# Half token tiles whose two parts share one stationary operand, and one expert's gathered rows turned later

## The chip, the cores and the metric

The kernel runs on one core of one Trainium2 chip. The time is device microseconds (us) of one execution; a run's figure is the median of several. Engines are named as in the profile: PE (TensorE matmul), PEld (its weight loads), DVE (VectorE), ACT (ScalarE), POOL (GpSimd) and SP (SyncE, which issues most DMAs).

## The reference

Three layers follow one another. A banded attention (2 batches, 8 heads, 768 tokens, 64 values a head) gives x of 2 x 768 tokens with 512 values each. A mixing layer with one hidden layer of 2048 changes x. The last layer sends each token to one of 8 experts, chosen by a gate, and the change touches only this one:

```python
for b in range(B):
    for s in range(S):
        ...
        h = np.maximum(x[b, s] @ w1[e], 0.0)      # 512 -> 1024
        out[b, s] = p[e] * (h @ w2[e])            # 1024 -> 512
```

## The kernel before

Every matrix product of the last two layers is made of three products. A number is kept as two parts, a high one (`xh`, `wh`, `hh`) and a low one (`xl`, `wl`, `hl`, the rest), and `three` (L601 to L604) adds high x high, high x low and low x high into one PSUM tile.

The experts are handled in ten positions one after the other: two filler positions (-2 and -1), then positions 0 to 7. `WIDTHS` fixes how many tokens each of the positions 0 to 7 has: 192, 256, 128, 192, 128, 192, 128, 192. `TILES` counts the tiles of 128 tokens that cover them, so widths of 192 and 256 have two tiles. For a width of 192 the second tile begins at token 64 (`at_tile`, L1109): tokens 64 to 127 are computed in both tiles and stored twice with the same values.

A position has four units (`NP2`), and each unit has two chunks c of 128 of the 1024 hidden values, so a position has eight chunks f. One chunk of a position with two tiles goes through `e_gemm1` (L844): twelve matmuls into `g`, weights stationary and 192 or 256 tokens moving, and then `split_relu` (ACT writes `hh`, DVE writes `hl`). One chunk later `out_` (L1256) multiplies hh and hl, as stationary operands, with 512 columns of the second weights: three matmuls of 512 columns per tile, into the accumulators z of tile 0 and z of tile 1. A position of one tile (width 128) works otherwise: x is stationary, the hidden values are turned on PE (`turn_`, L1214), copied by ACT (L1218) and subtracted by DVE (L1219), and six matmuls of 512 columns follow.

Around a position stand these steps, in the order written in `before` (L1160) and in `unit` (L1197):
- `listed` and `gathered` read the list of tokens and gather their rows of x by an indirect DMA that POOL issues (L803). `gathered(pos + 1)` is called in the first unit of position pos.
- `turned` (L1137, `split_x` L807) turns one gathered tile on PE (four transposes, L810), copies it (ACT, L813) and subtracts (DVE, L814). In the third unit of pos it turns tile 0 of pos + 1, in the fourth unit tile 1.
- `weights` loads 1 MB for each unit of the next position (L820), and `split_ew` cuts weights into two parts (ACT L837, DVE L840), four steps for each unit, handed out between other work.
- `done` (L1147) stores a position: `store` (L857) scales an accumulator on ACT (L861) and scatters its rows to the output by an indirect DMA of POOL (L862). The tile framework makes each scatter to the output wait until the scatter before it has landed.

In position 7 the second products of the chunks f = 4 to 7 are put off to the end of the program (L1334 to L1338), behind a branch that skips `past_tiles`: tile 0 with twelve matmuls and its store, then tile 1 with twelve and its store.

Of the kernel before, what the change touches and what calls it, by code (L numbers as in the profile page):

```python
# [22 lines left out]
P = 128  # L23
# [46 lines left out]
def tile_kernel(ctx, tc, q, k, v, nn, U, V, w12, wg, wgt, ew, masks, lst0, out, dbg=None):  # L70
# [736 lines left out]
    def split_x(xg, t, xh, xl, ps, nm, at=None):  # L807
# [8 lines left out]
    e_hl = {}  # L816

# [25 lines left out]

    def e_gemm1(key, f, w, xh, xl, between, room=None):  # L844
        wh, wl = e_hl[key, f // 2]
        c = f % 2
        hh, hl = room or [ep.tile([P, 256], F32R, tag=t, bufs=3, name=f"{t}{key}{f}") for t in ("ehh", "ehl")]
# [6 lines left out]
        split_relu(hh[:, :w], hl[:, :w], g[:, :w])  # L854
        return hh, hl

    def store(acc, idx, prob):  # L857
# [3 lines left out]
        nc.scalar.mul(ot, acc, prob)  # L861
# [247 lines left out]
    def at_tile(pos, t):  # L1109
        return min(P * t, WIDTHS[pos] - P)  # L1110

    def listed(pos):
# [9 lines left out]
        if WIDTHS[pos] % P:  # L1122
            for t in range(n):
                read_list(nc.sync.dma_start(ids[:, t], lst[ds(s_of[pos] + at_tile(pos, t), P), :]))
# [4 lines left out]
    def gathered(pos):  # L1129
        ids = ex[pos]  # L1130
        idc = ep.tile([P, 2], I32, tag="idc", bufs=3, name=f"idc{pos}")
        xh = ep.tile([P, KC, 256], F32R, tag="xh", name=f"xh{pos}")
        xl = ep.tile([P, KC, 256], F32R, tag="xl", name=f"xl{pos}")
        xs = [gather(ids[:, t, 0:1], idc[:, t:t + 1], x2d) for t in range(TILES[pos])]
        ex[pos] = ids, xh, xl, xs

    def turned(pos, t):  # L1137
        if t < TILES[pos]:
            ids, xh, xl, xs = ex[pos]
            split_x(xs[t], t, xh, xl, side_tile, f"{pos}{t}", at_tile(pos, t))  # L1140
# [6 lines left out]
    def done(pos, tiles=None):  # L1147
# [4 lines left out]
        else:  # L1152
            ids = ex[pos][0]
            for t in tiles or range(TILES[pos]):
                store(accs[pos][t], ids[:, t, 0:1], ids[:, t, 1:2].bitcast(F32))
# [4 lines left out]
    def before(pos, p):  # L1160
        if pos >= 0:
# [8 lines left out]
            if pos + 1 < E and p >= 2:  # L1170
                turned(pos + 1, p - 2)
# [25 lines left out]
    def unit(pos, p, key, xh, xl, n, acc_):  # L1197

        wh, wl = e_hl[key, p]
        if n == 1:  # L1200
# [10 lines left out]
            hh = ep.tile([P, 256], F32R, tag="ehh", bufs=3, name=f"ehh{key}{p}")  # L1211
            hl = ep.tile([P, 256], F32R, tag="ehl", bufs=3, name=f"ehl{key}{p}")
# [237 lines left out]
```

## Time and profile before

| what | value |
|---|---|
| median of 3 runs | 607.74 us (605.58 to 607.93) |
| the profiled execution, its own time | 607.19 us |
| its span, first to last instruction | 605.3 us |
| PE busy | 582.0 us, 96% of the span |
| DVE, ACT, POOL busy | 416.8, 292.0, 128.1 us |
| mean granted TensorE clock | 0.993 of full speed |
| positions 0 to 7 | from about 443 us to the end |

The time of an execution is its span and 1.9 us around it. PE is busy nearly throughout; in the expert positions it stands still in two places only. An engine's busy time counts the stretches in which it has an instruction under way; matmuls overlap in the records, so what one costs is the distance from its start to the start of the next.

### The profile page before, as it was taken

To read this page: it belongs to the slowest core of one execution; us is meant where nothing else is said; L and a number is where in the kernel's file an instruction comes from. 1 tells how busy PE (TensorE), PEld (TensorE's weight loads), DVE (VectorE), ACT (ScalarE), POOL (GpSimd) and SP (SyncE) were. 2 spreads that over 40 slices of the span, in tenths; PEclk is the share of its full clock that TensorE was granted. 3 is DMA by queue.
4 is the path that set the end of the run, shared out by engine and by line. 5 is a ranking of instruction groups with operands and counts; after the bars stand their busy time and mean duration, and the time that the engine had idled before them with its cause. 6 is when DMAs were issued, how large, how long until landed. Compare 5 with 4: busy or idle time off the path is not lost. (4 is left out here: it accounts for less than half of the span.)

```text
span 605.3 us, 9730 instructions
## 1 busy us (share of the span) xinstructions
PE 582.0 (96%) x3469; PEld 518.1 (86%) x3469; DVE 416.8 (69%) x998; ACT 292.0 (48%) x631; POOL 128.1 (21%) x119
## 2 busy tenths in 40 slices
PE   8999999899999999999998999999899999999994
PEld 5999899789988899899997889877788989999993
DVE  5789986476899883448999445568624677595850
ACT  4877877633432342332222125425424677685841
POOL 5010030112213333333330211012330313031101
PEclk9999999989999999999999999999999999999998
DMA  8956651003323310250100028034295578868400
GB/s 216 311 157 198 217 172 50 2 5 134 140 91 118 140 69 1 88 191 36 36 18 0 1 65 317 37 122 157 54 359 199 178 266 323 275 244 310 167 15 35
DMA packets 35850, 83.47 MB, mean 138 GB/s; under 512 B 5631, under 2 KB 17791, under 8 KB 33744
## 3 DMA queue, kind: packets, MB, share of 16 engines
q1 hardware_dynamic: 31632, 70.87, 35.2%
q0 software_dynamic: 2784, 7.62, 3.5%
q10 hardware_dynamic: 1376, 4.26, 1.9%
q8 instruction: 29, 0.48, 0.3%
q14 instruction: 29, 0.24, 0.1%
HBM read 74.34 MB, written 8.77 MB: 137 GB/s over the span
## 5 line engine op out<-in xcount | busy, mean ns | idle before, releaser
L607 ACT ACTIVATE hh<-g 128x384 fp32r<-128x384 f32 x62 | 30.3, 489 | 109.0 <-PE g L604 108.5
L608 DVE SCALAR_TENSOR_TENSOR hl<-g,hh 128x384 fp32r<-128x384 f32 x62 | 34.5, 556 | 48.6 <-ACT hh L607 48.3
L338 PE MATMUL s<-kt,q 128*128 128x232 f32 (+1 forms) x192 | 55.2, 370 | 2.3 <-DVE m L348 1.7
L352 ACT ACTIVATE e<-t,m 128x232 f32<-128x232 f32 (+1 forms) x96 | 45.6, 476 | 18.2 <-DVE m L348 17.7
L675 DVE CUSTOM_DVE_ANT_0 sq_w<-x,wgt 128x512 f32<-128x512 f32 x54 | 47.1, 872 | 1.4
L348 DVE CUSTOM_DVE_ANT_0 t<-s,bias 128x232 f32<-128x232 f32 (+1 forms) x96 | 36.0, 377 | 17.2 <-PE s L338 7.2
L217 ACT ACTIVATE sq_w<-w 128x512 f32<-128x512 f32 x32 | 21.5, 672 | 48.9 <-DVE wf L224 48.9
L862 POOL DMA_INDIRECT out_dram<-x,ids x13 | 13.6, 1048 | 121.5 <-ACT x L861 100.6
L365 ACT COPY et<-pt 128x256 f32<-128x256 f32 (+1 forms) x96 | 33.5, 349 | 6.0 <-PE pt L362 3.8
L362 PE MATMUL pt<-ident,e 128*128 128x128 f32 x176 | 35.0, 273 | 0.0
L338 PEld LDWEIGHTS s<-kt,q 128*128 128x128 f32 x192 | 29.7, 191 | 5.4 <-DVE m L348 3.9
L222 DVE SCALAR_TENSOR_TENSOR wf<-w,wf 128x512 int32<-128x512 int32 x32 | 32.5, 1017 | 0.8
L382 PE MATMUL o<-v,et 128*128 128x65 f32 x160 | 30.9, 275 | 0.0
L783 POOL DMA_INDIRECT lst<-tab,slot x12 | 12.6, 1047 | 78.2 <-DVE tab L779 77.1
L608 DVE SCALAR_TENSOR_TENSOR ehlr<-egr,ehhr 128x192 fp32r<-128x192 f32 (+1 forms) x28 | 10.6, 377 | 26.1 <-ACT ehhr L607 26.1
L362 PEld LDWEIGHTS pt<-ident,e 128*128 128x128 f32 x176 | 24.1, 142 | 4.3 <-ACT et L365 0.5
L381 PE MATMUL o<-v,et 104*128 104x65 f32 x160 | 26.9, 249 | 0.0
L220 DVE SCALAR_TENSOR_TENSOR wf<-w,wf 128x512 int32<-128x512 int32 x32 | 25.6, 800 | 1.1 <-DVEq L463 0.7
L381 PEld LDWEIGHTS o<-v,et 104*128 104x128 f32 x160 | 24.2, 191 | 0.8
L382 PEld LDWEIGHTS o<-v,et 128*128 128x128 f32 x160 | 24.3, 191 | 0.0
L607 ACT ACTIVATE ehhr<-egr 128x192 fp32r<-128x192 f32 (+1 forms) x28 | 9.7, 347 | 29.1 <-PE egr L604 27.6
L224 DVE SCALAR_TENSOR_TENSOR wf<-sq_w,wf 128x512 f32<-128x512 f32 x32 | 22.1, 691 | 1.7
(777 smaller groups left out, 1935.8 us busy)
## 6 DMA issues: line engine op xcount, KB each, us to landing
ew<-in_ew_dram SPq DMA_DIRECT2D x32, 1024.0 KB, 6.4
w<-in_w_dram SPq DMA_DIRECT2D x16, 1024.0 KB, 4.8
v<-in_v_dram SPq DMA_DIRECT2D x8, 704.0 KB, 5.2
ew<-in_ew_dram ACTq DMA_DIRECT2D x4, 1024.0 KB, 11.7
x2d<-x SPq DMA_DIRECT2D x12, 256.0 KB, 2.0
kt<-in_k_dram SPq DMA_DIRECT2D x7, 408.0 KB, 4.1
q<-in_q_dram SPq DMA_DIRECT2D x14, 192.0 KB, 4.5
wgt<-in_wgt_dram SPq DMA_DIRECT2D x4, 512.0 KB, 4.3
```

The source lines that it names most:

```text
L220: nc.vector.scalar_tensor_tensor(t, low, 29, t, ALU.logical_shift_right, ALU.bitwise_or)
L222: nc.vector.scalar_tensor_tensor(t, high, -0x40000000, t, ALU.bitwise_and, ALU.bitwise_or)
L338: nc.tensor.matmul(s[:, :w], qs[n % 2][:, c], kt[:, kc], start=True, stop=True)
L348: nc.vector.tensor_tensor_reduce(out=t[:, :w], in0=s[:, :w], in1=bias[:, h, b0:b0 + w], scale=-0.125, scalar=3.0e38, op0=ALU.add, op1=ALU. ...
L352: nc.scalar.activation(e[:, :w], t[:, :w], AF.Exp, bias=m, scale=-1.0)
L362: nc.tensor.transpose(pt[:, P * j:P * j + P], e[:, c0:c0 + P], ident)
L365: nc.scalar.copy(et[:, :w], pt[:, :w])
L381: nc.tensor.matmul(oo, et[0:REST, 0:P], vt[0:REST, NT + i - 1, vc], start=True, stop=False)
L382: nc.tensor.matmul(oo, et[:, P:256], vt[:, i, vc], start=False, stop=True)
L607: nc.scalar.activation(hi, src, AF.Relu)
L608: nc.vector.scalar_tensor_tensor(lo, src, 0.0, hi.bitcast(F32), ALU.max, ALU.subtract)
L675: nc.vector.tensor_tensor_reduce(out=sq_w, in0=x_t[0, i], in1=rooms[k % 2][:, DM * j:DM * j + DM], scale=1.0, scalar=0.0, op0=ALU.mult, op ...
```

## The change

Positions with 192 tokens (0, 3, 5 and 7) get a second tile of 64 tokens in place of one of 128. Its list, its gather, its four transposes, its copy and subtraction and its store are of 64 rows (`tile_rows`). The two parts hh and hl of a chunk now lie in one tile `hl2` of 512 columns: hh in the first 192, the hl of tile 0 from column 256, and the hl of the half tile directly behind its hh, in columns 192 to 255. So the half tile's 64 columns of hh and 64 of hl are one stationary operand of 128 columns: `both` multiplies it with the high weights in one matmul (hh x high into rows 0 to 63 of the accumulator, hl x high into rows 64 to 127), and a second matmul with a stationary operand of 64 columns adds hh x low weights to rows 0 to 63. The two halves of the accumulator are added at the store: ACT copies the lower half, DVE adds, DVE scales, and POOL scatters 64 rows. The hl of 192 tokens is written by two DVE instructions (128 and 64 columns). At the end of the program the half tile is now multiplied and stored first, the tile of 128 behind it.

The second part of the change concerns position 1 alone: its gathered tile 0 is turned in the fourth unit of position 0 in place of the third, and tile 1 in the middle of that fourth unit.

```diff
-    def gather(col, idc, src):
+    def gather(col, idc, src, n=P):
...
-        xg = x_t[0, rows["n"] % NT]
+        xg = x_t[0, rows["n"] % NT][0:n]
...
-            nc.tensor.transpose(tr[:, P * kk:P * kk + P], xg[:, P * kk:P * kk + P], ident)
-        trv = tr.rearrange("p (k c) -> p k c", k=KC)
-        c = slice(P * t, P * t + P) if at is None else slice(at, at + P)
+            nc.tensor.transpose(tr[:, P * kk:P * kk + n], xg[:, P * kk:P * kk + P], ident[0:n, 0:n])
+        trv = tr.rearrange("p (k c) -> p k c", k=KC)[:, :, 0:n]
+        c = slice(P * t, P * t + n)
...
+    HALF = P // 2
+
+    def tile_rows(pos, t):
+        return min(P, WIDTHS[pos] - P * t)
...
+    def second_products(acc, hl2, wh, wl, c, pos, t, start, stop):
+
+        w2h, w2l = wh[:, c, 512:], wl[:, c, 512:]
+        if tile_rows(pos, t) == P:
+            s_ = slice(P * t, P * t + P)
+            three(acc, hl2[:, s_], hl2[:, 256 + P * t:256 + P * t + P], w2h, w2l, start, stop)
+        else:
+            both = lambda: nc.tensor.matmul(acc, hl2[:, P * t:P * t + P], w2h, start=start, stop=stop)
+            if start:
+                both()
+            nc.tensor.matmul(acc[0:HALF], hl2[:, P * t:P * t + HALF], w2l, start=False, stop=False)
+            if not start:
+                both()
...
-        hh, hl = room or [ep.tile([P, 256], F32R, tag=t, bufs=3, name=f"{t}{key}{f}") for t in ("ehh", "ehl")]
+        hl2 = ep.tile([P, 512], F32R, tag="ehhl", bufs=3, name=f"ehhl{key}{f}") if room is None else room
...
-        split_relu(hh[:, :w], hl[:, :w], g[:, :w])
-        return hh, hl
+        nc.scalar.activation(hl2[:, :w], g[:, :w], AF.Relu)
+        full = w // P * P
+        for at, to, n in ((0, 256, full), (full, w, w - full)):
+            if n:
+                nc.vector.scalar_tensor_tensor(
+                    hl2[:, to:to + n], g[:, at:at + n], 0.0, hl2[:, at:at + n].bitcast(F32), ALU.max, ALU.subtract)
+        return hl2
...
-    def store(acc, idx, prob):
+    def store(acc, idx, prob, n=P):
...
-        nc.scalar.mul(ot, acc, prob)
+        if n == P:
+            nc.scalar.mul(ot, acc, prob)
+        else:
+            ot = ot[0:n]
+            lower = ep.tile([n, 512], F32, tag="lower", bufs=1, name=f"lower{rows['o']}")
+            nc.scalar.copy(lower, acc[n:2 * n])
+            nc.vector.tensor_tensor(lower, acc[0:n], lower, ALU.add)
+            nc.vector.tensor_scalar(ot, lower, prob, None, ALU.mult)
...
-            if pos + 1 < E and p >= 2:
-                turned(pos + 1, p - 2)
+            if pos + 1 < E and p >= (2 if pos else 3):
+                turned(pos + 1, p - (2 if pos else 3))
...
                     for t in range(n):
-                        s_ = slice(at_tile(pos, t), at_tile(pos, t) + P)
-                        three(acc_[t], hh[:, s_], hl[:, s_], wh[:, c, 512:], wl[:, c, 512:], f == 0, f == FC2 - 1)
+                        second_products(acc_[t], hl2, wh, wl, c, pos, t, f == 0, f == FC2 - 1)
                         after(t == 0)
...
                 second()
+                if (pos, p, c) == (0, NP2 - 1, 0):
+                    turned(1, 1)
                 state["out"] = out_
...
-    for t in range(TILES[E - 1]):
-        for f, c, hh, hl, wh, wl in end[1:]:
-            s_ = slice(at_tile(E - 1, t), at_tile(E - 1, t) + P)
-            three(accs[E - 1][t], hh[:, s_], hl[:, s_], wh[:, c, 512:], wl[:, c, 512:], False, f == FC2 - 1)
+    for t in reversed(range(TILES[E - 1])):
+        for f, c, hl2, wh, wl in end[1:]:
+            second_products(accs[E - 1][t], hl2, wh, wl, c, E - 1, t, False, f == FC2 - 1)
         done(E - 1, [t])
```

On PE, the second products of one chunk of position 0 (its second chunk) stood like this before; `z_5024` is the accumulator of tile 0, `z_5025` that of tile 1, and the last row begins the next chunk's first products:

```order
L602 MATMUL z_5024<-er-1_0h,ehhr-11_5043 128x512
L603 MATMUL z_5024<-er-1_0l,ehhr-11_5043 128x512
L604 MATMUL z_5024<-er-1_0h,ehlr-11_5044 128x512
L602 MATMUL z_5025<-er-1_0h,ehhr-11_5043 128x512
L603 MATMUL z_5025<-er-1_0l,ehhr-11_5043 128x512
L604 MATMUL z_5025<-er-1_0h,ehlr-11_5044 128x512
L602 MATMUL egr-13_5093<-xh_4904,er-1_1h 128x192
```

After the change the same place on PE reads as follows (`z_5014` and `z_5015` are the two accumulators, `ehhlr` the common tile):

```order
L602 MATMUL z_5014<-er-1_0h,ehhlr-11_5033 128x512
L603 MATMUL z_5014<-er-1_0l,ehhlr-11_5033 128x512
L604 MATMUL z_5014<-er-1_0h,ehhlr-11_5033 128x512
L858 MATMUL z_5015<-er-1_0l,ehhlr-11_5033 64x512
L855 MATMUL z_5015<-er-1_0h,ehhlr-11_5033 128x512
L602 MATMUL egr-13_5080<-xx_4899,er-1_1h 128x192
```

One matmul of 512 columns has gone, and one of the two that are left for tile 1 has an output of 64 rows, between two matmuls with an output of 128 rows.

On PE, position 1's tile 0 was turned at the start of position 0's third unit (`gt_5114`), behind the second products of its third chunk:

```order
L602 MATMUL z_5025<-er-1_1h,ehhr-12_5068 128x512
L603 MATMUL z_5025<-er-1_1l,ehhr-12_5068 128x512
L604 MATMUL z_5025<-er-1_1h,ehlr-12_5069 128x512
L810 MATMUL gt_5114<-ident,x_68 128x128 x4
L602 MATMUL egr-14_5123<-xh_4904,er-1_2h 128x192
```

Now it stands (`gt_5154`) one unit further on, at the start of the fourth unit:

```order
L603 MATMUL z_5014<-er-1_2l,ehhlr-14_5101 128x512
L604 MATMUL z_5014<-er-1_2h,ehhlr-14_5101 128x512
L858 MATMUL z_5015<-er-1_2l,ehhlr-14_5101 64x512
L855 MATMUL z_5015<-er-1_2h,ehhlr-14_5101 128x512
L810 MATMUL gt_5154<-ident,x_68 128x128 x4
L602 MATMUL egr-16_5162<-xx_4899,er-1_3h 128x192
```

Two chunks of first products and of second products have moved ahead of the four transposes; nothing else has changed its place there.

On DVE, where position 3 is stored and position 4 (one tile) has begun, the subtraction that makes position 4's low part (`ehlr_6057`) stood between weight cuts:

```order
L840 TENSOR_TENSOR er_1l<-ew_1_5751,er_1h 128x512 x3
L840 TENSOR_TENSOR er_2l<-ew_2_5753,er_2h 128x512 x2
L1219 TENSOR_TENSOR ehlr_6057<-etr_6085,ehhr_6056 128x256
L840 TENSOR_TENSOR er_2l<-ew_2_5753,er_2h 128x512 x2
L840 TENSOR_TENSOR er_3l<-ew_3_5824,er_3h 128x512 x2
```

Now the two steps of the half tile's store stand ahead of it:

```order
L844 TENSOR_TENSOR er_1l<-ew_1_5721,er_1h 128x512 x3
L844 TENSOR_TENSOR er_2l<-ew_2_5723,er_2h 128x512 x2
L890 TENSOR_TENSOR lower_6032<-z_5726,lower_6032 64x512
L891 TENSOR_SCALAR x_69<-lower_6032,ids_5242 64x512
L1250 TENSOR_TENSOR ehhlr_6018<-etr_6048,ehhlr_6018 128x256
L844 TENSOR_TENSOR er_2l<-ew_2_5723,er_2h 128x512 x2
```

The subtraction has moved behind an addition and a scaling that wait for ACT's copy of the lower half of z. The same holds in position 6, behind position 5.

## Rows read from the trace of the kernel before

**Rows 1.** Busy time of each engine by stretch (us), granted clock, DMA share, GB/s

```profile
460.00:480.00 20.00, 20.00 (x134) 18.15 (x133) 12.56 (x23) 11.83 (x25) 4.05 (x6) 1.00 0.40 132
```

**Rows 2.** What PE waited for from 443 us on: total us, times, longest

```profile
PE gt L810 <- DMA x<-x2d,idc: 1.9, 1, 1.9
```

**Rows 3.** Timeline of PE at position 1's gathered rows: start, length (us), instruction

```profile
452.50 0.39 PE L603 MATMUL z<-er-1_1l,ehhr-12_5068 128*128 128x512 f32 x1
452.73 0.39 PE L604 MATMUL z<-er-1_1h,ehlr-12_5069 128*128 128x512 f32 x1
455.00 0.44 PE L810 MATMUL gt<-ident,x 128*128 128x128 f32 x2 [1.88 <-DMA x<-x2d,idc]
```

**Rows 4.** Timeline of POOL: the gather of position 1's tile 1

```profile
447.80 1.04 POOL L803 DMA_INDIRECT x<-x2d,idc  x1 [0.27 <-POOL idc L800]
```

**Rows 5.** DMA issues from 447 to 449 us, us from issue to landing

```profile
x<-x2d,idc POOLq DMA_INDIRECT x2, 8.7
```

**Rows 6.** Timeline of PE around matmuls with small stationary operands (rows*columns ahead of the output)

```profile
423.15 0.28 PE L604 MATMUL egr-23_4734<-ehr-2_3_4229,xfl 128*128 128x256 f32 x1
423.27 0.38 PE L1217 MATMUL etr-22_4741<-ident,ehr-22_4704 128*128 128x128 f32 x2
...
423.61 0.28 PE L603 MATMUL egr-23_4734<-elr-2_3_4230,xfh 128*128 128x256 f32 x1
...
424.06 0.28 PE L604 MATMUL egr-23_4734<-ehr-2_3_4229,xfl 128*128 128x256 f32 x1
424.27 0.39 PE L774 MATMUL sl<-tab,route 40*128 40x9 f32 x2
424.58 0.50 PE L1224 MATMUL z-20_4540<-ehr-2_2_4123,ehhr-22_4706 128*128 128x512 f32 x1
424.93 0.39 PE L1225 MATMUL z-20_4540<-elr-2_2_4124,ehhr-22_4706 128*128 128x512 f32 x1
425.25 0.19 PE L792 MATMUL cn<-ident,cum 8*1 8x8 f32 x2
425.37 0.51 PE L1224 MATMUL z-20_4540<-ehr-2_2_4123,ehhr-22_4706 128*128 128x512 f32 x1
425.71 0.40 PE L1225 MATMUL z-20_4540<-elr-2_2_4124,ehhr-22_4706 128*128 128x512 f32 x1
```

**Rows 7.** Timeline of PE's weight loads at the same place

```profile
425.36 0.19 PEld L1224 LDWEIGHTS z-20_4540<-ehr-2_2_4123,ehhr-22_4706 128*128 128x128 f32 x1
425.47 0.19 PEld L1225 LDWEIGHTS z-20_4540<-elr-2_2_4124,ehhr-22_4706 128*128 128x128 f32 x1
```

**Rows 8.** Timeline of ACT, DVE and PE where position 3 is stored

```profile
528.09 1.27 ACT L861 ACTIVATE x<-z,ids 128x512 f32<-128x512 f32 x2
...
529.65 0.42 DVE L1219 TENSOR_TENSOR ehlr<-etr,ehhr 128x256 fp32r<-128x256 f32 x1 [1.26 <-ACT ehhr L1218]
...
530.72 0.63 PE L1228 MATMUL z<-er_0h,ehlr 128*128 128x512 f32 x2
```

**Rows 9.** Timeline of the last 14 us: PE's first, ACT's and POOL's instructions

```profile
592.46 0.50 PE L602 MATMUL z<-er_2h,end 128*128 128x512 f32 x1 [0.68 <-ACTq L1332]
...
595.55 0.69 ACT L861 ACTIVATE x<-z,ids 128x512 f32<-128x512 f32 x1 [3.41 <-PE z L604]
...
596.51 0.98 POOL L862 DMA_INDIRECT out_dram<-x,ids  x1 [17.36 <-ACT x L861]
...
598.34 0.69 ACT L861 ACTIVATE x<-z,ids 128x512 f32<-128x512 f32 x1 [2.10 <-PE z L604]
599.97 0.98 POOL L862 DMA_INDIRECT out_dram<-x,ids  x1 [2.47 <-ACT x L861]
```

**Rows 10.** DMA issues from 590 us to the end, us to landing

```profile
out_dram<-x,ids POOLq DMA_INDIRECT x2, 2.7
```

**Rows 11.** Groups of DVE instructions by form: busy us, mean ns

```profile
L500 DVE TENSOR_TENSOR x<-mx,x 128x512 f32<-128x512 f32 x12 | 8.2, 686 | 1.0 <-PE mx L499 0.8
L218 DVE TENSOR_SCALAR wf<-w 128x512 int32<-128x512 int32 x32 | 13.5, 421 | 0.0
```

More of the change, by code (lines that the diff above doesn't have):

```diff
@@ L1123, in listed @@
             for t in range(n):
[L1124 removed]
+                r = tile_rows(pos, t)
+                read_list(nc.sync.dma_start(ids[0:r, t], lst[ds(s_of[pos] + P * t, r), :]))
         else:
@@ L1131, in gathered @@
         idc = ep.tile([P, 2], I32, tag="idc", bufs=3, name=f"idc{pos}")
[L1132 to L1135, printed above, removed]
+        xx = ep.tile([P, KC, 2, 256], F32R, tag="xx", name=f"xx{pos}")
+        xs = []
+        for t in range(TILES[pos]):
+            r = tile_rows(pos, t)
+            xs.append(gather(ids[0:r, t, 0:1], idc[0:r, t:t + 1], x2d, r))
+        ex[pos] = ids, xx, xs
     def turned(pos, t):
         if t < TILES[pos]:
-            ids, xh, xl, xs = ex[pos]
-            split_x(xs[t], t, xh, xl, side_tile, f"{pos}{t}", at_tile(pos, t))
+            ids, xx, xs = ex[pos]
+            split_x(xs[t], t, xx[:, :, 0], xx[:, :, 1], side_tile, f"{pos}{t}", tile_rows(pos, t))
     def weights(pos, p):
@@ L1154, in done @@
             for t in tiles or range(TILES[pos]):
-                store(accs[pos][t], ids[:, t, 0:1], ids[:, t, 1:2].bitcast(F32))
+                n = tile_rows(pos, t)
+                store(accs[pos][t], ids[0:n, t, 0:1], ids[0:n, t, 1:2].bitcast(F32), n)
     units = [(pos, p) for pos in range(-2, E) for p in range(NP2)]
@@ L1210, in unit @@
             nc.scalar.activation(h, g[:, :256], AF.Relu)
-            hh = ep.tile([P, 256], F32R, tag="ehh", bufs=3, name=f"ehh{key}{p}")
-            hl = ep.tile([P, 256], F32R, tag="ehl", bufs=3, name=f"ehl{key}{p}")
+            hl2 = ep.tile([P, 512], F32R, tag="ehhl", bufs=3, name=f"ehhl{key}{p}")
+            hh, hl = hl2[:, :256], hl2[:, 256:]
             def turn_():
@@ L1248, in unit @@
                     end.append(wf_tile("end", F32R))
-                hh, hl = e_gemm1(key, f, WIDTHS[pos], xh, xl, turn, [end[0][:, w, 256 * (f % 4):256 * (f % 4) + 256] for w in range(2)] if late_f else None)
+                room = end[0][:, f % 4 // 2, 512 * (f % 2):512 * (f % 2) + 512] if late_f else None
+                hl2 = e_gemm1(key, f, WIDTHS[pos], xh, xl, turn, room)
                 after(True)
@@ L1252, in unit, with out_ @@
                     second()
-                    end.append((f, c, hh, hl, wh, wl))
+                    end.append((f, c, hl2, wh, wl))
                     continue
-                def out_(f=f, c=c, hh=hh, hl=hl):
+                def out_(f=f, c=c, hl2=hl2):
                     for t in range(n):
-                        s_ = slice(at_tile(pos, t), at_tile(pos, t) + P)
-                        three(acc_[t], hh[:, s_], hl[:, s_], wh[:, c, 512:], wl[:, c, 512:], f == 0, f == FC2 - 1)
+                        second_products(acc_[t], hl2, wh, wl, c, pos, t, f == 0, f == FC2 - 1)
                         after(t == 0)
@@ L1282, in tile_kernel @@
         else:
-            _, xh, xl, _ = ex[pos]
-            xh, xl = xh[:, :, :WIDTHS[pos]], xl[:, :, :WIDTHS[pos]]
+            xx = ex[pos][1][:, :, :, :WIDTHS[pos]]
+            xh, xl = xx[:, :, 0], xx[:, :, 1]
         split_until(u)
@@ L1310, in past_tiles @@
                 read_list(nc.sync.dma_start(ids[:, 0], lst[ds(s_r + t * P, P), :]))
-                xh = ep.tile([P, KC, 256], F32R, tag="xh", name="oxh")
-                xl = ep.tile([P, KC, 256], F32R, tag="xl", name="oxl")
+                xx = ep.tile([P, KC, 2, 256], F32R, tag="xx", name="oxx")
+                xh, xl = xx[:, :, 0], xx[:, :, 1]
                 xg = gather(ids[:, 0, 0:1], idc[:, 0:1], x2d)
```

8 lines of the change are left out of this document (3 added, 5 removed).

## The prediction

> **What bounds the kernel now.** I began with the busy times by stretch: in the expert positions PE is busy for 20.00 of 20 us, while DVE has 12.56 and ACT 11.83, and the granted clock is 1.00, so 2.4 GHz [rows 1]. Then I asked what PE waits for from 443 us on. Only one wait bears on the change, 1.9 us for gathered rows of x [rows 2]; the other, 0.68 us at the branch near the end, stays as it is [rows 9]. So until about 592 us the time is the sum of what PE executes, and a matmul saved there is worth the distance from one start to the next: 0.23 us for 512 columns [rows 3]. The last 14 us are different. ACT's first scaling ends at 595.55 + 0.69 = 596.24, and the scatter starts 0.27 later. The second scaling ends at 599.03, but its scatter starts only at 599.97 [rows 9]. The first scatter takes 2.7 us to land [rows 10], so it landed at 599.2, and the second, which must wait for it, starts 0.77 later. The end of the program therefore hangs on when the first of the two stores is issued, not on PE's last matmul.
>
> **The change part by part.** Six steps.
>
> **A, second products.** Each of the four positions of 192 tokens has eight chunks; four of position 7's are in the tail, so 28 chunks lie in the stretch that PE bounds. Each drops one of six matmuls: 28 x 0.23 = 6.5 us saved, if the rest keeps its pace. But one of the five that are left has a stationary operand of 64 columns between operands of 128. No row of before has that shape, so I bound it. Below, nothing: a matmul of 512 columns takes its 0.23 whatever stands still. For the other side I looked for places where the stationary operand fills only part of the array. Two matmuls with an operand of 8 rows x 1 column: from the start of the matmul ahead (424.93) to the end of the slot of the one behind (425.71) is 0.78 us, where two matmuls of 512 columns and two tiny ones (about 0.05 together) should take 0.51. The excess is 0.27. Two with 40 rows: from 424.06 to 424.93 is 0.87, where a matmul of 256 columns (0.12), two paced by their weight loads (0.11 each, the distance of two loads in rows 7) and one of 512 (0.23) make 0.57. The excess is 0.30. As a control, two transposes with a full operand: 423.15 to 423.61 is 0.46, and 0.12 + 2 x 0.11 + 0.12 is 0.46, so no excess [rows 6]. It is the partial operand that costs, once going in and once coming out. Coming out, the weight load of the next matmul starts with the matmul itself (425.36 and 425.37) and takes the 0.11 until the next load [rows 6, 7]: it isn't hidden, as loads are elsewhere. Going in, the same should hold for 64 columns, about half of 0.11. So I take 0.27 + 0.05 = 0.32 for each half tile, with 0.20 (the load coming out hidden) and 0.41 (0.30 and a whole load) as bounds beside nothing. 0.32 paid for 0.23 saved is 0.09 lost: 28 x 0.09 = **+2.5 us**, between -6.5 and +5.0.
>
> The Trainium skill speaks against this change more plainly. Its page "TensorEngine Tiling (Array Packing)", under Tiling Modes, lists 128x64 as a configuration of its own beside 128x128, and says under Key Properties that a change of the mode, not only of the tile, drains TensorE. Taken at its word it rules out the lower bound of nothing; no row here shows a 64-column operand, so I keep that case as a rival.
>
> **B, four transposes of 64 rows** in each of four places. Their operand has 64 rows, so by the same rows they pay about 0.30; the transposes are paced by their loads and gain nothing. At position 0 they stand next to a wait of PE for ACT, which should hide it: 3 x 0.30 = **+0.9 us**, between 0 and +1.2.
>
> **C, position 1's rows turned later.** The turn issues four transposes, one ACT copy and one DVE subtraction for each tile, no DMA; its gathers on POOL and the loads on the DMA queues keep their places. PE's matmul before the wait has its slot until 452.73 + 0.23 = 452.96 and the transposes start at 455.00 [rows 3], so 2.0 us are lost. In the new place PE has two chunks more to do first, each at least 12 x 0.11 (first products can't outrun their loads) and 5 x 0.23, together 5.0 us: it comes at 458 or later. Tile 1's gather was issued at 447.80 and takes 8.7 us [rows 4, 5], so it is there at 456.5, and tile 0's at 455.0. Tile 1 is now turned 2.5 us (twelve first products and five second ones) ahead of position 1's first matmul; copy and subtraction need 1.3 us, and DVE and ACT have room [rows 1]. So **-2.0 us**.
>
> **D, the tail.** From PE's start there (592.46) the first scatter came 4.05 us later: twelve matmuls (2.78), 0.31 until ACT starts, 0.69, and 0.27 to POOL [rows 9]. Now the half tile is first: eight matmuls (1.86), four times 0.32 less the 0.09 of the first entry, which falls in idle time, make 3.05; then 0.31, ACT's copy 0.69, DVE's addition (0.69, as the addition from PSUM with 512 columns) and scaling (0.42, the nearest one-input form) [rows 11], and 0.27: 5.43. The last scatter waits for that store, lands 2.7 + 0.77 behind it as before, and the large tile's own scaling is long done by then. 1.4 us later, less 0.1 for half the rows: **+1.3 us**; +0.2 if the narrow operand costs nothing. The four matmuls saved here bring nothing, since PE's end isn't what counts.
>
> **E, the stores of positions 3 and 5.** DVE's addition and scaling, 1.11 us, wait for ACT's copy, and behind them on DVE stand the subtraction that PE needs for position 4's (and 6's) low products, and weight cuts. ACT's two stores end at 529.36. DVE then subtracted at 529.65 for 0.42, to 530.07, and PE used it at 530.72 [rows 8], so 0.65 were spare. Now DVE is free at 530.47 and done at 530.9: 0.2 late, twice, **+0.4 us**; between 0 and 1.4 if more cuts stand in between. On POOL the half tile's scatter waits for DVE too, and the next position's gathers queue behind it; they have a whole position's time. At position 0 no such subtraction is near.
>
> **F, at nothing:** the second DVE instruction for hl (28 times at most the 0.36 of one of 192 columns) lies in DVE's idle 7 us of 20 [rows 1]; without that cover it would cost up to 10 us. Smaller gathers and lists move too little to count.
>
> Sum: 2.5 + 0.9 - 2.0 + 1.3 + 0.4 = +3.1 us. The profiled execution took 607.2, so 610.3. It lies 0.55 below the median of the runs; splitting that, I say **610.5 us**.
>
> **The rivals.**
> 1. *The narrow operand costs nothing* (the side of faster). A -6.5, B 0, C -2.0, D +0.2, E +0.3: -8.0, 599.2. For it: all rows with an excess have few rows or few columns, none has 64 columns and all rows. Against it: both kinds seen cost alike, 0.27 and 0.30. It decides where the price is under 0.23 a chunk by much; at 0.23 A is zero.
> 2. *A price of 0.20*, because the next load is hidden behind 512 moving columns where it couldn't hide behind 8. A -0.8, B +0.6, C -2.0, D +0.9, E +0.4: -0.9, 606.3. For it: longer streams give more cover. Against it: the load waits for the drain, not for the stream.
> 3. *A price of 0.41 and DVE late by 0.7 at both stores*: A +5.0, B +1.2, C -2.0, D +1.7, E +1.4: +7.3, 614.5.
> 4. *The wait of C isn't gone*, because the loads of position 1's weights hold up the gathers further: +2.0 on the forecast, 612.5. Against it: 1.5 us of margin at least.
>
> **How the numbers follow.** Chances: forecast 0.44, rival 1 0.27, rival 2 0.14, rival 3 0.12, rival 4 0.03. The forecast alone spans 608 to 613 (a price of 0.27 to 0.38). A measurement of this kernel can tell about 0.5%, 3 us, from no change: 604.7 and 610.8 are the borders. Rival 1 is faster (0.27); rivals 3 and 4 are slower (0.15), and 0.20 of the forecast; the rest, 0.24 of the forecast and rival 2, is within: 0.38. The range from 598.5 to 613.0 holds the forecast nearly whole, two thirds of rival 1 (597.5 to 601.5) and rival 2, about 0.8.
>
> **What would show it.** In the profile after: the half tile's row L858 starts some 0.3 us after the matmul ahead of it in place of 0.23, and the full-size matmul behind it (L855) keeps a slot of 0.34 or more; a chunk of position 0 has second products of 1.48 us in place of 1.39. If the five stand 0.23 apart, A is wrong and rival 1 holds. No PE wait at L810 after 443 us shows C right. In the tail, the first scatter 5.4 us after PE's start shows D right, 4.2 rival 1. A wait of PE for DVE's L1250 in positions 4 and 6 shows E.

## The result and the profile after

The changed kernel takes **599.8 us** (median of 4 runs, 599.42 to 600.51) against 607.84 us (4 runs, 605.58 to 608.55) for the kernel before on the same chip: a ratio of **0.9861** with a 95% interval of 0.9818 to 0.9905. The forecast was 610.5 us, so its sign was wrong. The time is that of rival 1, the narrow operand that costs nothing, for which 599.2 us had been worked out with a chance of 0.27; it lies inside the range, near its lower end. The profiled execution of the changed kernel took 599.84 us with a span of 598.0 us.

The profile page's line of busy times, which answers to the table of before:

```profile
PE 575.3 (96%) x3437; PEld 509.7 (85%) x3437; DVE 421.7 (71%) x1038; ACT 291.1 (49%) x631; POOL 128.8 (22%) x119
```

PE is busy for 6.7 us less and is still 96% of the span. What PE waits for from 443 us on (total us, times, longest) answers to [rows 2]:

```profile
PE z L1255 <- ACT ehhlr L1249: 0.6, 2, 0.3
PE z L858 <- PEq L1365: 0.6, 1, 0.6
```

The 1.9 us for gathered rows have gone. A wait of twice 0.3 us for ACT's L1249 is new; it comes ahead of the second products of the first unit of positions 4 and 6. In a position of one tile a unit's two chunks go together, and its second products stand in the next unit. Next, PE's second products of one chunk of position 0 (start, length, instruction), the place that the first two listings of the change show:

```profile
448.53 0.39 PE L604 MATMUL z<-er-1_0h,ehhlr-11_5033 128*128 128x512 f32 x1
448.76 0.39 PE L858 MATMUL z<-er-1_0l,ehhlr-11_5033 128*64 128x512 f32 x1
448.99 0.39 PE L855 MATMUL z<-er-1_0h,ehhlr-11_5033 128*128 128x512 f32 x1
449.21 0.25 PE L602 MATMUL egr-13_5080<-xx,er-1_1h 128*128 128x192 f32 x1
```

The row with 128*64 is the narrow operand. Its start is 0.23 after the start ahead of it, the full operand behind it follows 0.23 later, and the next row 0.22 after that. No price shows here, going in or coming out. The tail answers to [rows 9]; engines are mixed here, in order of time:

```profile
585.16 0.45 PE L858 MATMUL z<-er_2l,end 128*64 128x512 f32 x1 [0.58 <-PEq L1365]
...
587.27 0.58 ACT L889 COPY lower<-z 64x512 f32<-64x512 f32 x1 [2.33 <-PE z L855]
...
588.60 0.48 DVE L891 TENSOR_SCALAR x<-lower,ids 64x512 f32<-64x512 f32 x1
...
589.36 0.92 POOL L892 DMA_INDIRECT out_dram<-x,ids  x1 [16.44 <-DVE x L891]
...
590.05 0.69 ACT L885 ACTIVATE x<-z,ids 128x512 f32<-128x512 f32 x1 [2.19 <-PE z L604]
592.62 0.98 POOL L892 DMA_INDIRECT out_dram<-x,ids  x1 [2.34 <-issue]
```

The first scatter starts 589.36 - 585.16 = 4.20 us after PE's start there, against 4.05 before [rows 9]. The last one starts 3.26 behind the first, though its own data were scaled at 590.74.

To see where the time went, I cut the spans at PE's first matmul of each position's first products. The last chunk's second products of a position fall in the stage of the next, since they come one chunk later. Lengths in us:

| stage | before | after | difference |
|---|---|---|---|
| until position 0 starts | 443.42 | 442.89 | -0.53 |
| position 0 | 23.43 | 19.66 | -3.77 |
| position 1 | 22.77 | 22.56 | -0.21 |
| position 2 | 12.99 | 13.13 | +0.14 |
| position 3 | 22.54 | 20.88 | -1.66 |
| position 4 | 12.99 | 13.58 | +0.59 |
| position 5 | 22.56 | 20.88 | -1.68 |
| position 6 | 13.01 | 13.87 | +0.86 |
| position 7 until PE's start in the tail | 18.75 | 17.70 | -1.05 |
| tail, from there to the end | 12.85 | 12.80 | -0.05 |

The stretch ahead of position 0 is the same work in both; in the profiles of this study it ends anywhere from 441.7 to 443.8 us, so its 0.53 isn't the change's. All stages together make -7.4, the difference of the spans. Positions 4 and 6, which have no half tile of their own but store the one of the position before, became longer.

### The profile page after: what moved, and what is told of

Same layout as the page of the kernel before. It is cut to its first block, busy times and chain, and to the rows that moved or that the text cites. A ratio compares the mean times of both kernels' runs of the same rounds, so it can differ in the third digit from the quotient of the medians.

```text
span 598.0 us, 9718 instructions
## 1 busy us (share of the span) xinstructions
PE 575.3 (96%) x3437; PEld 509.7 (85%) x3437; DVE 421.7 (71%) x1038; ACT 291.1 (49%) x631; POOL 128.8 (22%) x119
## 5 line engine op out<-in xcount | busy, mean ns | idle before, releaser
L381 PE MATMUL o<-v,et 104*128 104x65 f32 x160 | 26.9, 249 | 0.0
L876 DVE SCALAR_TENSOR_TENSOR ehhlr<-egr,ehhlr 128x128 fp32r<-128x128 f32 (+2 forms) x48 | 11.8, 281 | 20.3 <-ACT ehhlr L872 19.4
L381 PEld LDWEIGHTS o<-v,et 104*128 104x128 f32 x160 | 24.2, 191 | 0.8
L872 ACT ACTIVATE ehhlr<-egr 128x192 fp32r<-128x192 f32 (+1 forms) x28 | 9.7, 346 | 26.0 <-issue 12.9
```

The costliest lines, as they stand in the source:

```text
L381: nc.tensor.matmul(oo, et[0:REST, 0:P], vt[0:REST, NT + i - 1, vc], start=True, stop=False)
```

## The experiments

Time in us (median, lowest to highest, runs), and the ratio to the kernel before on the same chip; where there is no ratio, there was one run.

| kernel | time | ratio, 95% interval |
|---|---|---|
| the changed kernel again | 599.90 (599.17 to 600.92, 6) | 0.9885 [0.9860, 0.9911] |
| second half product with 128 columns | 599.82 (599.19 to 600.67, 5) | 0.9881 [0.9863, 0.9900] |
| the same with 32 columns | 600.96 (1) | |
| position 1's turn alone | 604.79 (603.93 to 605.96, 9) | 0.9966 [0.9950, 0.9981] |
| half tiles alone | 603.76 (601.43 to 605.08, 7) | 0.9945 [0.9925, 0.9966] |
| tail in the old order | 600.11 (599.56 to 600.58, 5) | 0.9885 [0.9867, 0.9904] |
| gathered tiles turned whole | 599.60 (598.38 to 600.78, 6) | 0.9883 [0.9857, 0.9908] |
| half tile's store one unit later | 599.70 (598.88 to 600.55, 6) | 0.9884 [0.9858, 0.9909] |
| the two edits above together | 599.19 (598.80 to 599.83, 6) | 0.9873 [0.9848, 0.9898] |
| half tile's store by DVE alone | 598.47 (597.74 to 599.20, 4) | 0.9855 [0.9835, 0.9875] |
| half tile's store by ACT alone | 598.09 (1) | |
| store by DVE alone, tiles turned whole | 598.02 (596.52 to 598.23, 5) | 0.9846 [0.9831, 0.9861] |

Differences under 1 us are hard to tell by these times. Stage lengths repeat far better: position 3, which only the half tile's products touch, lasted 20.87 to 20.90 us in eleven of the twelve profiles of kernels with half tiles, and 20.93 in the other. So I read the small terms from stages.

The changed kernel was run again beside others, as a measure of how well its time and its stages repeat:

> The changed kernel once more, as the standard for the three kernels beside it. Every theory: 599.8 us, within 0.7.

It gave 599.90, with stage lengths within 0.06 us of those of the first profile.

**Does the narrow operand cost anything?** In one kernel it has the full width:

```diff
-            nc.tensor.matmul(acc[0:HALF], hl2[:, P * t:P * t + HALF], w2l, start=False, stop=False)
+            nc.tensor.matmul(acc, hl2[:, P * t:P * t + P], w2l, start=False, stop=False)
```

> The half tile's second matmul takes all 128 columns as its stationary operand in place of 64, so the low parts times the low weights are added too; the number of matmuls is that of the changed kernel. Theory 'free columns' (narrowing a stationary operand from 128 to 64 columns costs nothing beyond the slot of 0.23 us): the time of the changed kernel, 599.8 us, within 0.5, and the three spacings around the half tile stay at 0.23. Rival 'hidden price' (the narrow operand still costs some part of the 0.32 us that I forecast, spread over the matmuls around it): faster than the changed kernel by 28 times that part, so 2 us or more at 0.07 a chunk.

Time and stages are those of the changed kernel: positions 0, 3 and 5 last 19.69, 20.90 and 20.90 us. In a second kernel it is half as wide again:

```diff
-            nc.tensor.matmul(acc[0:HALF], hl2[:, P * t:P * t + HALF], w2l, start=False, stop=False)
+            nc.tensor.matmul(acc[0:32], hl2[:, P * t:P * t + 32], w2l, start=False, stop=False)
```

> The changed kernel, with the half tile's second matmul narrowed to 32 columns (for half of its tokens the product of high part and low weights is left out); the number of matmuls is the same. It asks whether it is the number of columns that the prediction got wrong. Theory 'columns never cost, only rows do': the spacings around it stay at 0.23 us and the time at 599.8 us. Rival '64 columns are a special case, 32 columns cost as the trace showed for an operand of 8 columns': 0.09 us more going in and 0.1 to 0.2 coming out, at 28 chunks that count, so 605 to 608 us.

Its timeline of PE at the place shown above:

```profile
449.44 0.40 PE L604 MATMUL z<-er-1_0h,ehhlr-11_5033 128*128 128x512 f32 x1
449.68 0.40 PE L858 MATMUL z<-er-1_0l,ehhlr-11_5033 128*32 128x512 f32 x1
449.91 0.40 PE L855 MATMUL z<-er-1_0h,ehhlr-11_5033 128*128 128x512 f32 x1
450.15 0.25 PE L602 MATMUL egr-13_5080<-xx,er-1_1h 128*128 128x192 f32 x1
```

The distances are 0.24, 0.23 and 0.24. Its one run took 600.96 us, but 0.9 of the 1.1 us above the changed kernel's profiled run lie ahead of position 0 (443.81 against 442.89), and from there on it is 0.2 longer in all; the rival wanted 5 us or more. With 128, 64 or 32 columns the slot is the same, so these three widths have no price here, with all 128 rows.

The weight loads on PEld show what the prediction's price was to come from, a load that can't run ahead of its matmul. In the changed kernel, at the place shown above:

```profile
448.53 0.13 PEld L858 LDWEIGHTS z<-er-1_0l,ehhlr-11_5033 128*64 128x64 f32 x1
448.76 0.19 PEld L855 LDWEIGHTS z<-er-1_0h,ehhlr-11_5033 128*128 128x128 f32 x1
```

The load of 64 columns starts 0.23 ahead of its matmul (448.76), and the full load behind it starts 0.23 ahead of its own (448.99). Both are hidden.

The trace of before also has two partial operands that the prediction's rows leave out. In the attention an operand of 104 rows stands between operands of 128 (PEld and PE in order of time):

```profile
110.66 0.30 PEld L381 LDWEIGHTS o<-v,et 104*128 104x128 f32 x2
110.77 0.33 PE L381 MATMUL o<-v,et 104*128 104x65 f32 x2
110.88 0.30 PEld L382 LDWEIGHTS o<-v,et 128*128 128x128 f32 x2
110.94 0.39 PE L382 MATMUL o<-v,et 128*128 128x65 f32 x2
```

Its load starts 0.11 ahead of its matmul, and the load behind it 0.06 ahead, the same leads as around operands of 128 rows there (L379: 53.96 for 54.07, and 54.18 for 54.24 behind it). It pays nothing. And in the gate an operand has all 128 rows but only 8 columns, in bf16:

```profile
344.40 0.40 PE L604 MATMUL y<-w14h,hl 128*128 128x512 f32 x1
...
344.72 0.20 PEld L757 LDWEIGHTS <-ab 128*8 128x8 bf16 x4 [0.36 <-issue]
344.72 0.39 PE L757 MATMUL ab<-tab,ab 128*8 128x128 bf16 x4
345.04 0.19 PEld L602 LDWEIGHTS g<-uth,w15h 128*128 128x128 f32 x1
345.04 0.45 PE L602 MATMUL g<-uth,w15h 128*128 128x384 f32 x1
```

This one does pay: it comes 0.32 after the matmul of 512 columns ahead in place of 0.23, its load starts only with its matmul, and so does the load behind it. So not every partial operand costs, and one with all its rows can. No run tells whether it is the 8 columns or the other number type.

**The two parts of the change apart.** The turn alone, on the kernel before:

```diff
-            if pos + 1 < E and p >= 2:
-                turned(pos + 1, p - 2)
+            if pos + 1 < E and p >= (2 if pos else 3):
+                turned(pos + 1, p - (2 if pos else 3))
...
+                if (pos, p, c) == (0, NP2 - 1, 0):
+                    turned(1, 1)
```

> The kernel before, with position 1's gathered rows turned one unit later and nothing else. Theory 'two separate gains' (the removed wait is worth 2.0 us and the dropped matmuls the rest): 605.7 us, 2.0 below the kernel before, and PE no longer waits for the gathered rows. Rival 'all from the turn' (the wait shifted later work by more than its own length): 600 to 602 us. Rival 'wait comes back elsewhere': 607.7 us with a new wait of PE of about 2 us in positions 0 or 1.

Position 0 fell from 23.43 to 21.35 us, by 2.08, and every other stage stayed within 0.05, apart from the stretch ahead of position 0. The kernel with half tiles and the old turn is the changed one with these lines taken back:

> The changed kernel, with position 1's rows turned where the kernel before turns them. Theory 'two separate gains': PE comes to the wait 0.7 us earlier (three half tiles of 0.23 are done by then), the gathered rows land when they did, so the wait is about 2.6 us and the time 599.8 + 2.7 = 602.5 us. Rival 'all from the turn': 606 us or more. Rival 'the gather itself is faster with fewer rows in the queues': a wait below 1.5 us and 601 us or less.

Its position 0 lasts 22.30, and PE's wait for gathered rows is longer than before the change:

```profile
PE gt L810 <- DMA x<-x2d,idc: 2.4, 1, 2.4
```

PE comes to the transposes earlier there, since it has fewer second products to do, and the rows land nearly when they did: the transposes start 11.38 us into position 0, against 11.57 before. So part of what the half tiles save in position 0 goes into the wait: they bring 23.43 - 22.30 = 1.13 there with the old turn and 21.35 - 19.66 = 1.69 with the new one. By the medians on that chip (606.98 for before) the parts alone bring 2.2 and 3.2 us, and together some 7 (the two kernels on that chip that keep both parts took 599.82 and 600.11). The stages make the difference smaller: between the half tiles alone and the changed kernel they show 2.64 in position 0 and no more than 0.03 in any other.

**Does the tail hang on the order of the two tiles?**

```diff
-    for t in reversed(range(TILES[E - 1])):
+    for t in range(TILES[E - 1]):
```

> The changed kernel, with the tile of 128 tokens multiplied and stored first at the end, as before, and the half tile last. Theory 'the tail hangs on two scatters in a row': the first scatter starts 4.05 us after PE's start there, lands 2.7 us later and the second follows at 7.5 us, when the half tile's longer chain (ACT copy, DVE addition and scaling) is ready at about 7.0; so the same time as the changed kernel, within 0.3 us. Rival 'the half tile's chain sets the end when it comes last': 0.5 to 1 us slower than the changed kernel.

The tail lasts 12.81 us, as with the half tile first (12.80). Its two scatters start at 589.98 and 593.42, 3.44 apart. The order is worth nothing.

**Do the transposes of 64 rows cost what the prediction took?** The gathered tile is turned with all 128 rows, the upper 64 of them rows that nobody reads:

```diff
-        xg = x_t[0, rows["n"] % NT][0:n]
+        full = x_t[0, rows["n"] % NT]
+        xg = full[0:n]
...
-        return xg
+        return full
...
-            nc.tensor.transpose(tr[:, P * kk:P * kk + n], xg[:, P * kk:P * kk + P], ident[0:n, 0:n])
+            nc.tensor.transpose(tr[:, P * kk:P * kk + P], xg[:, P * kk:P * kk + P], ident)
```

> The changed kernel, but the half tile's four transposes take all 128 rows of the gathered tile (the lower 64 hold older rows, whose columns aren't copied). Theory 'narrowing the rows costs, narrowing the columns doesn't': in the changed kernel the four transposes with 64 rows take 0.94 us from the matmul ahead to the next but one behind, against 0.79 with 128 rows; here it is 0.79 again at all places, and the time falls by 3 times 0.15, 0.4 us, to 599.4. Rival 'any narrower operand costs nothing': no change in these spacings.

Position 2 went from 13.13 to 12.98, position 4 from 13.58 to 13.45, position 6 from 13.87 to 13.70. The timeline of PE and its weight loads at one of the places in position 4, first the changed kernel (four transposes of 64 rows; x4 and x2 are instructions drawn into one row):

```profile
528.62 0.62 PE L1259 MATMUL z<-er_1h,ehhlr 128*128 128x512 f32 x2
...
529.17 0.32 PEld L810 LDWEIGHTS gt<-ident,x 64*128 64x128 f32 x4 [0.36 <-issue]
529.17 0.46 PE L810 MATMUL gt<-ident,x 64*128 64x64 f32 x4
...
529.56 0.19 PEld L602 LDWEIGHTS egr<-er_3h,xx 128*128 128x128 f32 x1
529.56 0.39 PE L602 MATMUL egr<-er_3h,xx 128*128 128x256 f32 x1
...
529.78 0.28 PE L603 MATMUL egr<-er_3l,xx 128*128 128x256 f32 x1
```

and the kernel that turns all 128 rows:

```profile
527.45 0.63 PE L1260 MATMUL z<-er_1h,ehhlr 128*128 128x512 f32 x2
...
527.69 0.59 PEld L811 LDWEIGHTS gt<-ident,x 128*128 128x128 f32 x4
527.92 0.60 PE L811 MATMUL gt<-ident,x 128*128 128x128 f32 x4
528.25 0.19 PEld L602 LDWEIGHTS egr<-er_3h,xx 128*128 128x128 f32 x1
528.27 0.36 PE L602 MATMUL egr<-er_3h,xx 128*128 128x256 f32 x1
...
528.48 0.28 PE L603 MATMUL egr<-er_3l,xx 128*128 128x256 f32 x1
```

From the first row's start to the transposes it is 0.55 with 64 rows and 0.47 with 128; from there to the L602 0.39 and 0.35; its slot is 0.22 and 0.21. In all 0.13, and 0.13 to 0.17 by the stages.

This sum hides a larger price. The transposes of 64 rows stand closer together: from the first to the last start it is 0.24 against 0.33, a gain of 0.09. From the last start to the L602 it is 0.15 against 0.03. So the price is 0.08 going in and about 0.14 coming out, 0.22 together, and 0.09 of it comes back. The loads agree: with 64 rows the load starts with its matmul, and so does the full load behind the group, while with 128 rows they start 0.23 and 0.02 ahead. The edit changes two things, the operand's rows and the transposes' moving columns. Going in, the two loads behind the same matmul differ only in their rows, 64 against 128; what has which part in the 0.14 coming out isn't told.

At position 0 the price is hidden, as the prediction said. From the transposes of the hidden values ahead of the group to the second products behind it, which wait for ACT, it is 0.84 us in both kernels (440.54 to 441.38 with 64 rows, 439.51 to 440.35 with 128).

**Why did positions 4 and 6 grow?** I first put the half tile's store one unit later, away from the position's first chunk:

```diff
+                if n < P and pos + 1 < E and TILES[pos + 1] == 1 and not tiles:
+                    state["half"] = lambda t=t: done(pos, [t])
+                    continue
                 store(
...
     def second():
+        half = state["half"]
...
+        if half is not None:
+            state["half"] = None
+            half()
```

> The changed kernel, but the half tiles of positions 3 and 5 are stored one unit later, behind the copy and the subtraction that PE waits for in the positions of one tile that follow. Theory 'the store's chain costs 1.6 us' (positions 4 and 6 lose 0.67 and 0.93 us against the kernel before, once the dropped matmul and the transposes are taken out): those losses go and the time is 598.2 to 598.8 us, with no wait of PE for the copy there. Rival 'positions 4 and 6 are slower because ACT and DVE, not PE, pace them now': the loss moves by a unit and the time stays at 599.8, within 0.4.

Position 4's second unit fell from 4.19 to 3.44 us, but its third rose from 3.66 to 4.31; the whole position lost only 0.10 us (13.58 to 13.48), position 6 0.38 (13.87 to 13.49). ACT is late one unit further on. There the store's copy stands on ACT at 525.48, and L1256, the copy of hh for the next second products, comes only at 526.56; PE starts them at 527.00. So moving the store brings back only 0.10 and 0.38 us of what the two positions lose, and the rest has to be found in its steps. With the whole transposes too:

> Both edits together: transposes of 128 rows and the later store. If both theories hold, the gains add: 599.8 - 0.4 - 1.3 = 598.1 us. If ACT and DVE pace positions 4 and 6, 599.4 us.

This gave 599.19 us; positions 4 and 6 lasted 13.33 each. The two gains add in the stages, but they are small.

To tell ACT's step from DVE's, the next two kernels leave one of them out. DVE alone, which reads both halves from PSUM, scales the one, and scales and adds the other:

```diff
-            nc.scalar.copy(lower, acc[n:2 * n])
-            nc.vector.tensor_tensor(lower, acc[0:n], lower, ALU.add)
-            nc.vector.tensor_scalar(ot, lower, prob, None, ALU.mult)
+            nc.vector.tensor_scalar(lower, acc[n:2 * n], prob, None, ALU.mult)
+            nc.vector.scalar_tensor_tensor(ot, acc[0:n], prob, lower, ALU.mult, ALU.add)
```

> The half tile's store without ACT: DVE scales the lower half of the accumulator from PSUM, then scales the upper half and adds, two steps (about 0.48 and 0.68 us) that wait for no copy. Theory: the loss of the changed kernel at positions 4 and 6 comes from ACT, whose copy of 0.58 us stands between the scaling of the large tile and the copy that PE's second products wait for (L1249). Then position 4 falls from 13.58 to about 12.9 (12.99 before, less the dropped matmul 0.23, plus 0.15 for the transposes), position 6 from 13.87 to about 12.9, and no wait of PE for that ACT copy is left. The tail's first scatter comes 3.6 us after PE's start there in place of 4.2, and the tail falls from 12.8 to 12.2. Together about 2.2 us less: 597.7 us. Rival: DVE's two steps are the cause; they are as long as before, so positions 4 and 6 stay above 13.3, and only the tail gains: 599.3 us.

ACT alone:

```diff
-            lower = ep.tile([n, 512], F32, tag="lower", bufs=1, name=f"lower{rows['o']}")
-            nc.scalar.copy(lower, acc[n:2 * n])
-            nc.vector.tensor_tensor(lower, acc[0:n], lower, ALU.add)
-            nc.vector.tensor_scalar(ot, lower, prob, None, ALU.mult)
+            nc.scalar.mul(ot, acc[0:n], prob)
```

> The half tile's store with ACT alone: ACT scales the upper half (0.58 us, as its copy was) and DVE does nothing; the lower half of the accumulator, hl x high, is left out of the output. Theory (ACT's step is the cause): PE still waits 0.3 us for ACT's copy in the first chunk of positions 4 and 6; only the 0.13 us that DVE made it late goes, so position 4 falls from 13.58 to about 13.45 and position 6 from 13.87 to 13.5 to 13.7. Rival (DVE's steps are the cause): both fall to about 12.9. In both cases the tail's first scatter comes 3.0 us after PE's start there in place of 4.2, and the tail falls from 12.8 to 11.6.

| | changed | ACT alone | DVE alone |
|---|---|---|---|
| position 4 | 13.58 | 13.15 | 12.93 |
| position 6 | 13.87 | 13.16 | 12.91 |
| tail | 12.80 | 11.68 | 12.71 |

Without any loss the two positions should last 12.99 - 0.23 (the dropped matmul) + 0.15 (transposes) = 12.91. So DVE's two steps alone, which wait for no copy, cost nothing, ACT's step alone about 0.24, and both, one waiting for the other, 0.67 and 0.96. The timelines of the second products of position 4's first unit show how. The changed kernel:

```profile
522.05 0.69 ACT L885 ACTIVATE x<-z,ids 128x512 f32<-128x512 f32 x1
...
522.41 0.38 PE L1248 MATMUL etr<-ident,ehr 128*128 128x128 f32 x2
...
522.77 0.58 ACT L889 COPY lower<-z 64x512 f32<-64x512 f32 x1
...
523.38 0.37 ACT L1249 CAST ehhlr<-etr 128x256 fp32r<-128x256 f32 x1
523.38 0.68 DVE L890 TENSOR_TENSOR lower<-z,lower 64x512 f32<-64x512 f32 x1 [1.02 <-ACT lower L889]
...
523.80 0.50 PE L1255 MATMUL z<-er_0h,ehhlr 128*128 128x512 f32 x1 [0.29 <-ACT ehhlr L1249]
524.10 0.48 DVE L891 TENSOR_SCALAR x<-lower,ids 64x512 f32<-64x512 f32 x1
...
524.50 0.41 DVE L1250 TENSOR_TENSOR ehhlr<-etr,ehhlr 128x256 fp32r<-128x256 f32 x1
524.61 0.39 PE L1256 MATMUL z<-er_0l,ehhlr 128*128 128x512 f32 x1
...
524.97 0.50 PE L1259 MATMUL z<-er_0h,ehhlr 128*128 128x512 f32 x1
```

ACT alone:

```profile
522.58 0.69 ACT L885 ACTIVATE x<-z,ids 128x512 f32<-128x512 f32 x1
522.94 0.38 PE L1245 MATMUL etr<-ident,ehr 128*128 128x128 f32 x2
523.16 0.67 ACT L888 ACTIVATE x<-z,ids 64x512 f32<-64x512 f32 x1
...
523.73 0.36 ACT L1246 CAST ehhlr<-etr 128x256 fp32r<-128x256 f32 x1
...
524.14 0.50 PE L1252 MATMUL z<-er_0h,ehhlr 128*128 128x512 f32 x1
```

DVE alone:

```profile
522.53 0.75 DVE L889 TENSOR_SCALAR lower<-z,ids 64x512 f32<-64x512 f32 x1
522.55 0.38 PE L1247 MATMUL etr<-ident,ehr 128*128 128x128 f32 x2
...
523.32 0.74 DVE L890 SCALAR_TENSOR_TENSOR x<-z,ids,lower 64x512 f32<-64x512 f32 x1
523.48 0.46 PE L1254 MATMUL z<-er_0h,ehhlr 128*128 128x512 f32 x1
```

Compare the distance from PE's transposes of the hidden values to the first second product: 0.93 with DVE alone, where nothing waits, 1.20 with ACT alone, 1.39 in the changed kernel. ACT's step stands ahead of the copy of hh that PE needs. ACT's three steps start 0.72 and 0.61 apart in the changed kernel, 0.58 and 0.57 where the middle one is a scaling like the first, so a copy between them costs 0.18 more. (The copy reads the lower half of the accumulator and the scaling the upper, so it needn't be the kind of instruction that costs.) In the changed kernel DVE, which waited for that copy, then brings hl late as well: L1259 starts 0.36 after the matmul ahead of it in place of 0.23. Position 4's second unit, which holds all of this, lasts 4.19 us against 3.52 with DVE alone. Of these 0.67, 0.46 is the distance above and 0.13 the late L1259; the rest is spread over the other second products. Position 6's second unit loses 0.65 in the same way, and its third 0.29 more (3.94 against 3.65): there ACT's L1249 waits 0.67 us for a DVE weight cut (L844) by the profile, and PE's second products start at 562.33, 0.35 after the matmul ahead. Together this is the 1.6 us lost.

What was expected of DVE alone came true in positions 4 and 6, but the tail had been set too short: its steps from PSUM took 0.75 and 0.74, not 0.48 and 0.68. The first scatter came 3.91 after PE's start, the second at 7.17 (7.46 in the changed kernel), yet the tail became only 0.09 shorter. What took the other 0.2 behind the last scatter stays open. For ACT alone positions 4 and 6 lie between what the two theories gave.

The version with both gains, DVE's store and tiles turned whole:

> Store of the half tile by DVE alone and gathered tiles turned whole, with all 128 rows. Theory: what both give adds up. Against the changed kernel, positions 2, 4 and 6 lose the 0.15 us of the narrow transposes, positions 4 and 6 the 0.67 and 0.94 us of the late copy, the tail 0.6: 2.7 us, 597.2 us. Rival (DVE's steps are the cause): 0.45 for the transposes and 0.6 in the tail alone, 598.8 us.

It is the fastest of those with more than one run: 598.02 us, 0.9846. The stages from position 2 to 6 make 80.32 us against 82.34 in the changed kernel, so 2.0 us come from what the experiments name. The interval of its ratio only just touches that of the changed kernel's second series (from 0.9860 on) and lies inside that of the first (0.9818 to 0.9905); the stages tell the two kernels apart, the times hardly.

## Why the prediction was wrong

**A, the step that failed.** It said that a partial stationary operand costs, "once going in and once coming out", 0.32 in all, and that 64 columns would pay as the operands of 8 rows x 1 column and of 40 rows did [rows 6]. The saving of 28 matmuls was counted rightly: positions 3 and 5 each lost 0.24 for each of the seven dropped ones that fall in their stage, 28 of them make 6.6 us, and 6.5 was the figure. But the price was nothing, so A is -6.6, not +2.5: 9.1 us, nearly all of the 10.7 between forecast and result. The step that gave the price was a weight load that starts only with its matmul. Such loads exist, at 64 rows and at 128 rows x 8 columns in bf16, but at 64 columns both loads start 0.23 ahead. Both rows that I generalized from had few rows, and one of them also few columns. Neither had 64 columns with all rows, so neither bore on this shape; "both kinds seen cost alike" was taken as evidence that the kind doesn't matter, while rival 1 had named the difference. The same trace had a partial operand that pays nothing, that of 104 rows, which should have kept "it is the partial operand that costs" from standing. The widths 32, 64 and 128 settle the matter for themselves; what sets the price of the shapes that do pay stays open.

The Trainium skill's page "TensorEngine Tiling (Array Packing)" lists 128x64 and 128x32 as configurations of their own under Tiling Modes, and says under Key Properties that changing the mode drains TensorE. The prediction read this as ruling out a price of nothing; the timelines show slots of 0.23 to 0.24 on both sides of operands of 64 and 32 columns, and the measurement decides. Whether the mode stayed the same there or its change cost nothing, no run tells.

**B.** Its three places cost +0.15 us each, 0.45 in all, against the 0.9 predicted. The price of a partial operand is there, 0.22 a group where 0.30 had been taken; the four transposes are also closer together and give back 0.09, which the prediction had excluded ("gain nothing"). That position 0's group is hidden held.

**C** was right, in size and in mechanism: -2.0 predicted, -2.08 with the turn alone, and no wait at L810. With half tiles the wait would even have been 2.4.

**D** was wrong with A: without a price the first scatter comes at 4.20 (rival 1: 4.2), and the tail is 0.05 shorter, not 1.3 longer. (For rival 1 the terms of D give 4.24 against 4.05, less 0.1 for half the rows: +0.1, not the +0.2 stated.) Its mechanism holds in the main: the tail follows the first store. With ACT alone the first scatter came 3.06 after PE's start, 1.14 earlier, and the tail was 1.12 shorter; with DVE alone it came 0.29 earlier and the tail was only 0.09 shorter.

**E** had the right place and direction and was too small: +0.4 predicted with bounds of 0 and 1.4, about +1.6 measured. The prediction let only DVE be late, for hl. It missed that ACT's own step is in the same queue as the copy of hh (L1249), which had 0.05 to spare: in the trace of before it ended at 529.62 and PE used it at 529.67. The wait that the profile shows (L1255 for ACT's L1249) is for that copy, not for DVE's L1250, the sign that the prediction had named.

**F** held: no wait of PE for DVE's split (L876) stands among PE's waits after 443 us.

Rival 1's sum was -8.0: A -6.5, C -2.0, D +0.2, E +0.3. Measured it is A -6.6, B +0.45, C -2.0, D -0.05, E +1.6, together -6.6; the profiles differ by 6.8 from position 0 on and 7.4 in all. Of the 0.2 left, 0.1 is PE's stand at the branch ahead of the tail, 0.58 in place of 0.68 [rows 9]; the rest isn't placed. That rival 1's 599.2 us came so near the 599.8 measured is partly luck: its sum misses 1.2 us from position 0 on, and 0.5 of this is made up by the stretch ahead of position 0, which the change doesn't touch.

## What to carry to other kernels

Before a price is carried from one shape to another, list what differs (rows, columns, moving length) and look for a row in which only one of them does, and for one that speaks against the price, as the operand of 104 rows did here; where there is none, the case of no price deserves as much weight as the extrapolation. When a step is moved or added beside a chunk, follow every queue that it stands in: here the engine that copies for a later step was also the one whose next instruction the bound engine needed. A store that one idle-enough engine does alone can be better than one handed between two, even if its own steps are longer.

## What the runs showed of the hardware

- A stationary operand of 32 or 64 columns and 128 rows between operands of 128 columns: slots of 0.23 to 0.24 us for 512 moving columns, as for 128, and weight loads that start 0.23 ahead of their matmuls.
- An operand of 104 rows between operands of 128: its load starts 0.11 ahead of its matmul (L381). One of 128 rows x 8 columns in bf16: its load starts with its matmul, and so does the load behind it (L757); it comes 0.32 after a matmul of 512 columns.
- Four transposes of 64 rows with 64 moving columns: the group's row is 0.46 long against 0.60 for 128 rows, but its load starts only with its matmul, 0.08 later, and so does the load behind it; in all the group costs 0.13 to 0.17 us more than one of 128 rows.
- DVE's scaling of 64x512 took 0.48 from SBUF (L891 of the changed kernel) and 0.75 from PSUM (L889 of the kernel with DVE alone).
- ACT: a copy behind a scaling started 0.72 after it, a scaling behind a scaling 0.58 after it, the first being 128x512 and the second 64x512 both times.
